# Top-32 attention with an MLP behind it: the order of the attention units changed, with the first loads and shifts moved

## Chip, cores and metric

One core of one Trainium2 chip. The metric is the device time of one execution in microseconds; the median of several executions is compared. All data is 32-bit float, except that the two weight matrices of the MLP arrive as 64-bit floats and are converted on the chip.

## The reference

Attention over 8 batches, 8 heads, 576 rows and head width 64, in which each row keeps only its 32 highest scores; then, on the joined heads (512 columns), a layer norm, a two-layer MLP (512 to 2048 to 512) and a residual:

```
scores = scale * np.matmul(q, k.transpose(0, 1, 3, 2))
kth = np.partition(scores, -top_k, axis=-1)[..., -top_k:-top_k + 1]
scores = np.where(scores >= kth, scores, -1000000000.0)
attn = softmax(scores)                       # max, exp, sum, divide
x = np.matmul(attn, v)                       # to (B, S, H*D)
xn = (x - mu) / np.sqrt(var + 1e-06) * g_ln
out = x + np.maximum(xn @ w_ch1, 0.0) @ w_ch2
```

## The kernel before, in words

**Units.** The attention is cut into units. A unit is one batch, one pair of heads (four pairs, `hp` 0 to 3) and one tile of query rows `qt`: tiles 0 to 3 have 128 rows for each of the two heads, tile 4 (`J`) is the rest, the last 64 rows, of which both heads share one tile of 128 partitions. There are 128 full units and 32 rest units, 160 in all. A `Job` is what one group of units of one head pair shares: keys and queries turned, values, one buffer `pt` of turned weights, one product with the values.

**The order of jobs** (L1027 to L1034) was: batch 0 as three parts (tiles 0 and 1; tiles 2 and 3; the rest alone), every part for the four head pairs; batch 1 as tiles 0, 1 and then tiles 2, 3 with the rest in the same group; batches 2 to 7 as tiles 0, 1 with the rest, then tiles 2, 3. So the rest units of batches 1 to 7 stood one by one between full units, and those of batch 0 as a run of four (units 16 to 19).

**Steps.** The main loop (from L1215) has one pass, a step, for each n. Each engine gets its instructions in exactly this written order (`manual_schedule`). Step n does, among other things:

- scores of unit n+2 on TensorE (L404), copied out of PSUM by ScalarE (`take_scores`, L385);
- the mask of unit n-1: ScalarE (L459, L460, L496), then GpSimd's subtraction (L499) and its watch (L466);
- the selection of the 32 highest of unit n on VectorE (`select`, MAX8 L447 and L439, MATCH_REPLACE8 L433), and at its end the halving of unit n+1 (L425, L426);
- the exponentials (L507) and the turning of the weights of a unit one or two steps back;
- the values of a group whose turned weights are complete (`values`, L632 and L639, `lag` steps after its last unit), and their placing into the rows of x (L674, L651);
- in between, eight times a step, `fill()`: pieces of MLP work from a list `todo`.

**Turning the weights.** A unit's 128-row weights reach `pt` in one of two ways. Either TensorE turns them (L565, eight transposes of 128x128 for a full unit, and two ScalarE copies at L577), or the unit is `moved`: VectorE turns blocks of 32x32 (L538, two instructions), one DMA writes them to DRAM (L553) and four bring them back in place (L548). The piece at the ends is turned by TensorE either way (L599). Before the change (L1058), of the units from the fifth job on, every unit that is not a rest and not the last of its group was moved.

**The MLP.** When four head pairs of two tiles are done, a block of 256 rows is given (`gives`): it is centred, turned (L738), multiplied by w1 (L779, 64 matmuls), and by w2. The first block uses plain products (L818); the 17 later ones a form with seven products for eight (L936, 56 matmuls), for which sums are made on GpSimd (L866 to L872) and two combined forms of w2 are fetched from DRAM (L1006). Two of the 18 blocks are made of rest rows, of four batches each. `slot(n)` spreads what is in `todo`, and what is to come, evenly over the steps left until the next gifts.

**Weights.** 32 pieces of w1 and w2 are fetched and converted in steps -1 to 19: ScalarE (L163, L165, L168), GpSimd (L164, L170), VectorE (`shift`, L176), GpSimd (`join`, L182, L184). The first four pieces were shifted and joined at the start of step 0, ahead of unit 0's selection on VectorE and ahead of everything that step gives GpSimd. MLP work on a weight piece can't start before it is joined. After the plain block the forms are built, so the projections of the second block can start at step 28.

**Loads.** Keys and queries of a job come by eight DMAs (L302): keys from SP's queue, queries, for the first two jobs, from ScalarE's. VectorE turns them (L331). A second job of the same batch and head pair (`twin`) fetches the turned keys and late queries that the first has kept in DRAM (`keep_heads` L345, `fetch_heads` L352); each job loads its values (L319), and GpSimd copies two pieces of them (`fill_ends`, L324).

Of the kernel before, what the change touches and what calls it, by code (L numbers as in the profile page):

```python
# [21 lines left out]
J = 4  # L22
# [7 lines left out]
def compute(  # L30
# [12 lines left out]
    nc = tc.nc  # L43
    P = nc.NUM_PARTITIONS
    B, H, S, D = q.shape
# [5 lines left out]
    NHP = H // 2  # L51
# [5 lines left out]
    def pool(name, bufs, **kw):  # L57
        return ctx.enter_context(tc.tile_pool(name=name, bufs=bufs, **kw))
# [23 lines left out]
    opool = pool("o", 2)  # L82
    xtpool = pool("xt", 1)
    hpool = pool("h", NF // 2)
    turnedpool = pool("turned_kq", 2, space=bass.MemoryType.DRAM)
    hbmpool = pool("hbm", 4, space=bass.MemoryType.DRAM)
    formpool = pool("forms", 1, space=bass.MemoryType.DRAM)
    psps = pool("ps", 5, space=PSUM)
# [111 lines left out]
    batches = {}  # L200
# [4 lines left out]
    batches = {n: x for n, x in batches.items() if x}  # L205
# [4 lines left out]
    def weights(n, phase):  # L210

        now, coming = batches.get(n, []), batches.get(n + 1, [])
        if phase == 0:
            for x in coming if n < LATE else []:
                x.fetch()
            for x in now[0::2] if n < LATE else []:
                x.split()
        elif phase == 1:  # L220
            for x in now if n >= LATE else now[1::2]:
                x.split()
            for x in coming if n >= LATE else []:
                x.fetch()

    def join_weights(n):
        for x in batches.get(n - 1, []):
            x.join()
# [65 lines left out]
    def load(job, first, second, later=False):  # L294

        job.ins = {}
        for name, src, queue in (("k", k, first), ("q", q, second)):
            t = ldpool.tile([P, S], FP32, tag=name + "in", name=name + "in")

            def part(i, t=t, src=src, queue=queue):  # L300
                head, d0 = 2 * job.hp + i * 32 // D, i * 32 % D
                queue.dma_start(  # L302
                    t[i * 32 : (i + 1) * 32, :].rearrange("b (n a) -> b n a", a=32),
                    src[job.b, head, :, d0 : d0 + 32].rearrange("(n b) a -> b n a", b=32),
                )

            for i in range(P // 32):
                if later:
                    age = (4 * len(job.ins) + i) // 2
                    loads.add(lambda i=i, part=part: part(i), -age)  # L310
                else:
                    part(i)
            job.ins[name] = t
# [62 lines left out]
    def scores(u):  # L376

        u.made = [score_half(u, s) for s in range(2)]
        return u.made[0][0][:, HALF:]

    def take_scores(u):
        u.sc = scpool.tile([P, 2, S], FP32, tag="sc", name="sc")
        for t in range(len(u.tiles)):
            for s in range(2):
                nc.scalar.copy(  # L385
                    u.sc[:, t, s * HALF : (s + 1) * HALF], u.made[s][t][:, 0:HALF]
                )
# [25 lines left out]
    def halve(u):  # L413

        nt = len(u.tiles)  # L420
        u.lo = lopool.tile([P, 2, HALF], FP32, tag="lo", name="lo")
        u.hi = hipool.tile([P, 2, HALF + 8 * low_rounds], FP32, tag="hi", name="hi")
        a, b = u.sc[:, 0:nt, 0:HALF], u.sc[:, 0:nt, HALF:S]
        lo, hi = u.lo[:, 0:nt], u.hi[:, 0:nt, 0:HALF]
        nc.vector.tensor_tensor(hi, a, b, ALU.max)  # L425
        nc.vector.tensor_tensor(lo, a, b, ALU.min)  # L426
# [66 lines left out]
    def mask(u, t):  # L493
        if u.e is None:
            u.e = epool.tile([P, 2, S], FP32, tag="e", name="e")
        nc.scalar.activation(  # L496
            u.e[:, t], u.sc[:, t], AF.Relu, bias=u.edge[:, t : t + 1], scale=-STEEP
        )
        nc.gpsimd.tensor_tensor(u.e[:, t], u.e[:, t], u.sc[:, t], ALU.subtract)  # L499
# [56 lines left out]
    def turn(u):  # L556

        g = u.group
        i0 = place_of(u)
        q0 = i0 * 32  # L560

        def part(t):
            ps = turned()
            for c in range(J):
                nc.tensor.transpose(  # L565
                    ps[:, c * P : (c + 1) * P], u.e[:, t, c * P + t * R : (c + 1) * P + t * R],
                    ident[:],
                )
            if u.rest:
                both = ps[:].rearrange("p (c h n) -> p h c n", h=2, n=R)  # L570
                for h in range(2):
                    nc.scalar.copy(
                        g.blocks[:, h, i0 : i0 + R // 32],
                        both[:, h].rearrange("p c (i n) -> p i c n", n=32),
                    )
            else:
                nc.scalar.copy(  # L577
                    g.blocks[:, t, i0 : i0 + P // 32],
                    ps[:].rearrange("p (c i n) -> p i c n", c=J, n=32),
                )  # L580

        def last():
            turn_ends(u)()

        heads = () if u.moved else range(len(u.tiles))
        return [lambda t=t: part(t) for t in heads] + [last]
# [58 lines left out]
    def take_values(g):  # L645
        g.oT = otpool.tile([P, GQ], FP32, tag="oT", name="oT")
        nc.scalar.copy(g.oT[:, 0 : g.nq], g.av[:, 0 : g.nq])
# [376 lines left out]

    jobs = []  # L1027
    for b in range(B):
        parts = [[0, 1], [2, 3], [J]]
        if b:  # L1030
            parts = [[0, 1], [2, 3]]
            parts[b < 2].append(J)
        for qts in parts:
            jobs += [Job(b, hp, [qts]) for hp in range(NHP)]  # L1034
    units = []
    for j in jobs:
        j.groups = [Group(j, qts) for qts in j.groups]
# [8 lines left out]
    fresh = []  # L1046
# [8 lines left out]
    CONVERTING = max(n for n in batches if batches[n]) + 2  # L1055
    EARLY = jobs[NHP].first

    for u in units[EARLY:]:  # L1058
        u.moved = not u.rest and u is not u.group.units[-1]


    for j, after_j in zip(jobs, jobs[1:] + [None]):
# [14 lines left out]
    for j in jobs:  # L1077
        if j.hp == NHP - 1:
            b = j.b
# [26 lines left out]
    def at(i):  # L1106
        return units[i] if 0 <= i < N else None
# [92 lines left out]
        x.fetch()  # L1200
    turn_heads(fresh[0])
    nc.sync.dma_start(grow[:], g_ln.rearrange("(c p) -> c p", p=P))
    load(fresh[1], nc.sync, nc.scalar)
    scores(units[0])
    take_scores(units[0])
    halve(units[0])
    scores(units[1])
    take_scores(units[1])
# [3 lines left out]
    for n in range(END):  # L1212
# [8 lines left out]
        u, nxt, mk = at(n), at(n + 1), at(n - 1)  # L1221
# [3 lines left out]
        parts = turn(ex) if ex and not ex.moved else []  # L1225
# [7 lines left out]
        if quick:  # L1233
            values(g)
            take_values(g)
        for x in batches.get(n - 1, []):
            x.shift()
        spare = None
        for x in ahead:
# [4 lines left out]
        if mk:  # L1244
            prepare(mk)
            for t in range(len(mk.tiles)):
                mask(mk, t)
        join_weights(n)
        if mk and doubt is not None:
            watch(mk)  # L1250
        if plain_done[0] is not None and plain_done[0] < n - 1:
# [85 lines left out]
        if last_rest and last_rest.rest and last_rest.job.b % 2:  # L1337
            hp = last_rest.job.hp
# [9 lines left out]
            select(u, 3)  # L1348
        if nxt:
            halve(nxt)  # L1350
        weights(n, 1)
        if g and not quick and g.job.hp == NHP - 1:
            for qt in g.qts:
# [18 lines left out]
@with_exitstack  # L1372
def kernel(
    ctx: ExitStack,
    tc: tile.TileContext,
    *operands: bass.AP,
):
    nc = tc.nc
    doubt = ctx.enter_context(tc.tile_pool(name="doubt", bufs=1)).tile(
        [1, 1], I32, tag="doubt", name="doubt"  # L1380
    )
    compute(tc, *operands, low_rounds=1, doubt=doubt[:])
    again = nc.values_load(  # L1383
        doubt[:], min_val=0, max_val=1,
        skip_runtime_bounds_check_because="a comparison's result",
    )
    with tc.If(again > 0):
        compute(tc, *operands, low_rounds=2, doubt=None)
# [31 lines left out]
```

## Time and profile before

Seen in one profiled execution on the chip; the medians are from executions without a profile.

| what | value |
|---|---|
| median of 3 runs (lowest, highest) | 1628.69 us (1627.76, 1628.86) |
| the profiled execution's own time | 1625.28 us |
| its span, first to last instruction | 1623.1 us |
| busy: TensorE matmul, VectorE, ScalarE, GpSimd | 1486.5, 1370.2, 1058.0, 1030.9 us |
| DMA | 228.27 MB, mean 141 GB/s |
| start of step 28 (VectorE's halving of unit 28) | 314.1 us |
| start of steps 40, 60, 88, 148 | 416.0, 584.3, 825.2, 1358.7 us |

How to read it: "PE" is TensorE's matmul, "PEld" its weight loads, "DVE" VectorE, "ACT" ScalarE, "POOL" GpSimd, "SP" SyncE. L936 is line 936 of the kernel. Each f32 matmul of the program stands as two records of TensorE, each transpose as one. The ends of matmuls are modelled, and one record lasts longer than the distance to the next start, so TensorE's busy time is more than the work that it did. The number in front of each step's time above is read from the VectorE instruction L425, of which there is one for each unit.

### The profile page before, as it was taken

Reading aid. Unit: us, or ns where it says so; the run is one execution under the profiler, and the core shown is the slowest. Engines: PE = TensorE matmul, PEld = TensorE weight load, DVE = VectorE, ACT = ScalarE, POOL = GpSimd, SP = SyncE. Lnnn points to the kernel's source line nnn. Section 1 sums busy time; section 2 is a strip of 40 time slices with the busy share of each in tenths; the row PEclk is TensorE's granted clock in tenths of the full one; section 3 lists DMA queues with packets and bytes.
Section 4 is the critical chain, followed back from the end, with each engine's and each line's share of the span. In section 5 each row is a group of like instructions: output and inputs, shape, how many; then the busy total and the mean of one; then the engine's idle time right before and its main releaser. Section 6 shows DMA issues by size and latency. Waiting matters only on the chain. (4 is left out here: it accounts for less than half of the span.)

```text
span 1623.1 us, 27069 instructions
## 1 busy us (share of the span) xinstructions
PE 1486.5 (92%) x7770; PEld 1124.5 (69%) x7770; DVE 1370.2 (84%) x3971; ACT 1058.0 (65%) x2984; POOL 1030.9 (64%) x1489
## 2 busy tenths in 40 slices
PE   3579678689979899999999999999999999999997
PEld 2346346467757677777777777777777777778886
DVE  5997978989999999999999999999999989882000
ACT  5878765566757686777666767677677766763221
POOL 6878976855546565667566747576657574746244
PEclk9779989799989999999999999999999999999999
DMA  6625644444646456445564556546554554522211
GB/s 159 167 69 160 195 119 130 153 138 118 197 121 202 126 144 172 158 152 133 162 192 131 142 148 176 161 122 174 144 174 149 146 148 156 157 90 85 71 34 54
DMA packets 367206, 228.27 MB, mean 141 GB/s; under 512 B 248772, under 2 KB 337352, under 8 KB 367048
## 3 DMA queue, kind: packets, MB, share of 16 engines
q1 hardware_dynamic: 362312, 225.86, 48.5%
q8 instruction: 64, 1.05, 0.3%
q10 hardware_dynamic: 4736, 0.59, 0.2%
q14 instruction: 94, 0.77, 0.2%
HBM read 154.01 MB, written 72.35 MB: 139 GB/s over the span
## 5 line engine op out<-in xcount | busy, mean ns | idle before, releaser
L499 POOL TENSOR_TENSOR e<-e,sc 128x576 f32<-128x576 f32 x288 | 405.1, 1425 | 421.7 <-ACT e L496 323.9
L779 PE MATMUL hps<-xT,w 128*128 128x256 f32 x2304 | 542.1, 385 | 6.0 <-ACT xT L741 3.8
L779 PEld LDWEIGHTS hps<-xT,w 128*128 128x128 f32 x2304 | 430.3, 193 | 76.2 <-issue 10.8
L447 DVE MAX8 m<-hi 128x8 f32<-128x296 f32 (+1 forms) x1152 | 469.8, 442 | 0.1
L433 DVE MATCH_REPLACE8 hi<-m,hi 128x288 f32<-128x288 f32 (+1 forms) x864 | 377.1, 441 | 0.0
L936 PE MATMUL ops<-w,h 128*128 128x256 f32 x1360 | 322.4, 384 | 3.4 <-DMA w<-forms 3.4
L936 PEld LDWEIGHTS ops<-w,h 128*128 128x128 f32 x1360 | 254.0, 193 | 41.7 <-issue 5.0
L496 ACT ACTIVATE e<-sc,m 128x576 f32<-128x576 f32 x288 | 209.3, 769 | 90.1 <-PE scps L599 89.0
L507 ACT ACTIVATE e<-e,m 128x576 f32<-128x576 f32 x288 | 226.8, 790 | 32.3 <-POOL e L499 31.3
L385 ACT COPY sc<-scps 128x288 f32<-128x288 f32 x576 | 187.0, 402 | 63.3 <-POOL e L499 49.8
L425 DVE TENSOR_TENSOR hi<-sc 128x576 f32<-128x576 f32 (+1 forms) x160 | 134.3, 840 | 68.4 <-POOL watched L466 64.0
L802 ACT ACTIVATE h<-hps 128x512 f32<-128x512 f32 x144 | 87.3, 607 | 121.3 <-PE hps L779 120.7
L632 PE MATMUL av<-pt,vb 128*64 128x256 f32 (+2 forms) x1088 | 143.2, 405 | 0.8 <-ACT pt L604 0.6
L426 DVE TENSOR_TENSOR lo<-sc 128x576 f32<-128x576 f32 (+1 forms) x160 | 135.4, 846 | 0.0
L538 DVE STREAM_TRANSPOSE sc<-e 128x512 f32<-128x512 f32 x176 | 113.9, 682 | 22.3 <-ACT e L507 22.3
L404 PE MATMUL scps<-kT,late_qT 64*128 64x288 f32 (+3 forms) x832 | 123.4, 415 | 7.8 <-ACT sc L385 5.7
L936 PE MATMUL ops<-wt,s 128*128 128x256 f32 x544 | 128.7, 381 | 0.4 <-POOL s L866 0.4
L439 DVE MAX8 hi<-lo 128x8 f32<-128x288 f32 x288 | 117.5, 443 | 0.0
L404 PE MATMUL scps<-kT,qT 64*128 64x288 f32 x512 | 91.7, 470 | 24.8 <-DVE qT L331 23.5
L565 PE MATMUL tp<-ident,e 128*128 128x128 f32 x448 | 73.3, 291 | 44.6 <-ACT e L507 29.7
L936 PEld LDWEIGHTS ops<-wt,s 128*128 128x128 f32 x544 | 100.1, 190 | 16.0 <-issue 2.3
L404 PEld LDWEIGHTS scps<-kT,late_qT 64*128 64x128 f32 (+1 forms) x832 | 70.6, 169 | 58.0 <-issue 18.0
(107 smaller groups left out, 1846.5 us busy)
## 6 DMA issues: line engine op xcount, KB each, us to landing
turned<-sc SPq DMA_DIRECT2D x88, 512.0 KB, 2.9
pt<-turned SPq DMA_DIRECT2D x352, 128.0 KB, 2.8
w<-forms SPq DMA_DIRECT2D x136, 256.0 KB, 4.1
vb<-in_v_dram SPq DMA_DIRECT2D x68, 288.0 KB, 3.6
raw<-in_moe_w_ch_dram SPq DMA_DIRECT2D x32, 512.0 KB, 5.3
kT<-kept SPq DMA_DIRECT2D x36, 288.0 KB, 3.3
kin<-in_k_dram SPq DMA_DIRECT2D x128, 72.0 KB, 2.6
kept<-kT SPq DMA_DIRECT2D x32, 288.0 KB, 3.0
```

The lines of the kernel that those rows point to most:

```text
L385: nc.scalar.copy(u.sc[:, t, s * HALF : (s + 1) * HALF], u.made[s][t][:, 0:HALF])
L404: nc.tensor.matmul(ps[i * R : i * R + ql, o : o + width], qT[r, q0 : q0 + ql], kT[r, k0 : k0 + width], start=True, stop=True,)
L425: nc.vector.tensor_tensor(hi, a, b, ALU.max)
L426: nc.vector.tensor_tensor(lo, a, b, ALU.min)
L433: nc.vector.match_replace(x, m[:, t, :], x, LOWEST)
L447: nc.vector.max(m[:, t, :], u.hi[:, t, 0:width])
L496: nc.scalar.activation(u.e[:, t], u.sc[:, t], AF.Relu, bias=u.edge[:, t : t + 1], scale=-STEEP)
L499: nc.gpsimd.tensor_tensor(u.e[:, t], u.e[:, t], u.sc[:, t], ALU.subtract)
L507: nc.scalar.activation(u.e[:, t], u.e[:, t], AF.Exp, bias=u.bias[:, t : t + 1], scale=-scale, accum_out=g.den[:, col : col + 1],)
L632: nc.tensor.matmul(av[h * D : (h + 1) * D, 0 : g.nq], vb[:, h * (J + 1) + c, :], g.blocks[:, h, 0 : g.nq // 32, c, :], start=(c == 0), sto ...
L779: nc.tensor.matmul(ps[0][:, side * N : (side + 1) * N], w1[:, c, f * P : (f + 1) * P], self.xT[:, c, 0:N], start=(c == 0), stop=(c == NC - 1),
L936: nc.tensor.matmul(bank[name][:, 0:Q], a(j), rhs, start=first and j == 0, stop=(j == G - 1), skip_group_check=not first,)
```

## The change

- The order of jobs is written out. The rest rows of batches 0, 1, 2 and 3 are jobs of their own (runs of four rest units), and each run stands one or more parts behind its batch: batch 0's behind tiles 0, 1 of batch 2, batch 1's behind tiles 0, 1 of batch 3, batch 2's behind tiles 2, 3 of batch 3, batch 3's behind tiles 0, 1 of batch 4. Batches 4 and 5 have the rest with tiles 2, 3; batches 6 and 7 with tiles 0, 1, and the tiles 2, 3 of batches 6 and 7 come last.
- From the third batch on, the last unit of a group is moved as well (turned by VectorE), unless the next group begins with a rest unit, or it is a rest itself. The number of moved units goes from 88 to 103.
- Five instead of two DRAM buffers hold the kept keys and late queries of each head pair.
- The second job's loads are issued after the scores of unit 0 are copied, not before.
- The first four weight pieces are shifted and joined at the end of step 0, not at its start.

```diff
-    turnedpool = pool("turned_kq", 2, space=bass.MemoryType.DRAM)
+    turnedpool = pool("turned_kq", 5, space=bass.MemoryType.DRAM)
...
-    jobs = []
-    for b in range(B):
-        parts = [[0, 1], [2, 3], [J]]
-        if b:
-            parts = [[0, 1], [2, 3]]
-            parts[b < 2].append(J)
-        for qts in parts:
-            jobs += [Job(b, hp, [qts]) for hp in range(NHP)]
+    rows, rest = ([0, 1], [2, 3]), [J]
+    order = [(0, rows[0]), (0, rows[1]), (1, rows[0]), (1, rows[1])]
+    order += [(2, rows[0]), (0, rest), (2, rows[1]), (3, rows[0]), (1, rest)]
+    order += [(3, rows[1]), (2, rest), (4, rows[0]), (3, rest), (4, rows[1] + rest)]
+    order += [(5, rows[0]), (5, rows[1] + rest)]
+    order += [(6, rows[0] + rest), (7, rows[0] + rest), (6, rows[1]), (7, rows[1])]
+    assert B == 8
+    jobs = [Job(b, hp, [qts]) for b, qts in order for hp in range(NHP)]
...
-    for u in units[EARLY:]:
-        u.moved = not u.rest and u is not u.group.units[-1]
+    for j, nj in zip(jobs, jobs[1:] + [None]):
+        for u in units[max(j.first, EARLY) : j.last + 1]:
+            u.moved = not u.rest and (
+                u.i < j.last or (j.b > 1) and nj is not None and not units[nj.first].rest
+            )
...
-    load(fresh[1], nc.sync, nc.scalar)
     scores(units[0])
     take_scores(units[0])
+    load(fresh[1], nc.sync, nc.scalar)
...
-        for x in batches.get(n - 1, []):
+        for x in batches.get(n - 1, []) if n else []:
             x.shift()
...
-        join_weights(n)
+        if n:
+            join_weights(n)
...
         if nxt:
             halve(nxt)
+        if n == 0:
+            for x in batches[-1]:
+                x.shift()
+            join_weights(0)
         weights(n, 1)
```

## The prediction

> **What bounds the kernel now.** I read first the page's table of busy times and its forty slices: no engine is full over the whole span, TensorE (PE) is full from about slice 15 on, and VectorE (DVE) goes idle at slice 37.
>
> ```profile
> PE 1486.5 (92%) x7770; PEld 1124.5 (69%) x7770; DVE 1370.2 (84%) x3971; ACT 1058.0 (65%) x2984; POOL 1030.9 (64%) x1489
> PE   3579678689979899999999999999999999999997
> DVE  5997978989999999999999999999999989882000
> PEclk9779989799989999999999999999999999999999
> ```
>
> Second, the table by windows, cut at the starts of steps 28, 40, 60, 88 and 148 (columns: length, busy time of PE, PEld, DVE, ACT, POOL, granted clock, DMA share, GB/s).
>
> ```profile
> 314.10:416.00 101.90, 93.42 (x491) 69.88 (x491) 93.97 (x276) 69.15 (x206) 58.75 (x89) 0.93 0.48 145
> 416.00:584.30 168.30, 152.66 (x799) 112.66 (x796) 165.23 (x492) 114.50 (x338) 95.48 (x145) 0.95 0.56 158
> 584.30:825.20 240.90, 238.40 (x1302) 182.79 (x1302) 235.73 (x697) 170.28 (x502) 153.96 (x238) 1.00 0.55 155
> 825.20:1358.70 533.50, 532.20 (x2884) 410.38 (x2883) 505.75 (x1478) 373.13 (x1077) 345.61 (x525) 1.00 0.53 153
> 1358.70:1623.10 264.40, 253.34 (x1276) 208.67 (x1274) 105.14 (x312) 110.56 (x294) 131.19 (x223) 0.99 0.29 88
> ```
>
> Steps 28 to 60 are VectorE's (92 and 98% busy); then both are nearly full; at the end TensorE works alone. Third, since a matmul's busy time is modelled, TensorE's timeline, for the distance between starts:
>
> ```profile
> 1013.64 2.38 PE L632 MATMUL av<-pt,vb 128*64 128x320 f32 x16
> 1015.94 0.81 PE L639 MATMUL av<-pt,ends 128*128 128x320 f32 x2
> 1016.59 3.18 PE L936 MATMUL ops<-w,h 128*128 128x256 f32 x14
> ...
> 1559.49 1.04 PE L738 MATMUL tp<-ident,x 128*128 128x128 f32 x8
> 1560.36 0.60 PE L936 MATMUL ops<-w,h 128*128 128x256 f32 x2
> 1561.25 27.89 PE L779 MATMUL hps<-xT,w 128*128 128x256 f32 x128 [0.29 <-ACT xT L741]
> 1588.98 10.52 PE L936 MATMUL ops<-w,h 128*128 128x256 f32 x48
> ```
>
> 128 records in 27.73 us are 0.2166 us each, so 0.433 a matmul; a transpose is 0.87 / 8 = 0.109; a values product of 320 rows takes 2.95. Read in the same way, one of 256 rows takes 2.41 and one of 64 rows (at 216.7 us) 0.88; a score matmul 0.293. Priced so, TensorE's work from step 28 on is 1239.8 us (442.9 hidden, 411.7 projections, 151.0 scores, 145.1 values, 34.1 transposes L565, 55.0 others), while those steps took 1309.0. By stage: 85.5, 148.5, 232.9, 523.7, 249.1. So from step 60 to 148 TensorE is at 97 to 98% of that price: it is the bound there, whereas steps 28 to 60 hold 36 us in which it starves.
>
> **What the skill says.** "Perfetto Trace Analysis", Identifying the Most-Contended Engine: matmul busy time is a poor measure. The trace agrees: 532.20 of 533.50 us is shown against 523.7 priced by starts. "TensorE: Matmul & The Clock Gate", What's actually happening: an idle TensorE falls to half clock. The trace agrees in kind: 0.93 and 0.95 in the two starving stages, 1.00 after. "SBUF — State Buffer", Who interferes with whom: VectorE instructions with two SBUF inputs and GpSimd reads lock each other out. The trace agrees in kind: L425 takes 0.99 us at 314.1, 0.73 at 323.5. That is why I scale VectorE.
>
> **The change, part by part.** The order in which the changed kernel issues its instructions gives the counts.
>
> *Turned by VectorE.* 15 more units: TensorE loses 120 transposes, 120 x 0.109 = 13.1 us, ScalarE 30 copies (0.587 us each, 17.6 us; it has room), VectorE gains 30 transposes L538 at 0.678 (18 to 20 us), SP 75 DMAs (15 MB).
>
> *Rests alone.* Twelve groups of 320 rows become 256 and 64: 2.41 + 0.88 - 2.95 = 0.34 us, 4 us on TensorE. GpSimd gains 24 copies L324 at 0.23 us (6 us, hidden: it is 65% busy). SP's queue gains 36 loads (kept keys, late queries, values; 9 MB). With the other DMAs SP has 111 more, 24 MB on 228; DMA share 0.53 in the middle, so I take nothing. What stands behind SP's waits is later loads, issued two steps ahead; if that cover goes, each late load costs up to its landing, about 3 us, and TensorE waits. `fill_ends` waits on TensorE's previous values, with the next mask behind it on GpSimd; before, this was seen once with a 3.6 us wait on TensorE.
>
> *Sum on TensorE from step 28:* 1228.9, which is 10.9 less.
>
> *Order.* Steps 16 to 19 were rests and become full units. Before, those took 41.5 us (186.0 to 227.5), the four full steps ahead of them 47.8 (138.2 to 186.0): +6.3. Two key turnings (1.4 us each) move ahead into steps 13 and 15; most of that returns later: +2. VectorE's extra work in steps 0 to 27 is 17.9 us, which is the upper end; zero the lower.
>
> *Early moves.* Queries' four DMA issues (2.99 us on ScalarE) no longer stand ahead of the first copies, and VectorE no longer waits for four shifts (it idles 7 us in step 0). But unit 2's halving waits for GpSimd's watch of unit 0 (40.3 us), which stands behind the same eight joins (10 us) as before. The gain is capped there: I take 1, bounds 0 and 7. New wait: joins behind the late shifts, with unit 0's masks behind them; GpSimd has piece five's two instructions meanwhile. Five DRAM buffers cost nothing: space alone.
>
> So step 28 starts at 314.1 + 6.3 + 2 - 1 = 321.4.
>
> *Stages from there.* VectorE's work before, priced by starts, was 88.3, 158.6, 224.5, 476.2 and its busy time 1.065, 1.042, 1.050, 1.062 times that; I keep the factors. TensorE gets 1.018 (533.5 / 523.7).
>
> - Steps 28 to 39: VectorE 109.5 x 1.065 = 116.6, TensorE 104.6. VectorE decides: 116.6.
> - 40 to 59: VectorE 162.7 x 1.042 = 169.5, TensorE 165.5; they alternate (four rests, then sixteen full units), so a little over: 171.
> - 60 to 87: TensorE 231.3 x 1.018 = 235.5, VectorE 206.
> - 88 to 147: TensorE 487, VectorE 470 x 1.062 = 499, but TensorE enters it behind, up to two steps; 492.
> - From 148: TensorE 251.8 against 249.1; 264.4 + 2.8 = 267.2.
>
> Sum 1282.3 for 1309.0. The span is 321.4 + 1282.3 = 1603.7; the time lay 2.2 above the span, so 1605.9 where the profiled run had 1625.3; the median lies 3.4 above that one: **1609**.
>
> What is late next is VectorE itself: its stages are within 3% of TensorE's.
>
> **The rivals.**
>
> *The front costs nothing* (full steps no slower, factors 1.04): 314 + 114 + 169 + 235.5 + 488.5 + 265 = 1586, so 1592. For it: the rests' steps 19 and 20 took 14.1 and 12.1 us, with stalls. Against: VectorE has 17.9 us more in there.
>
> *Stretches add instead of overlapping: slower.* A rest step wants some 9 us of TensorE and 4.8 of VectorE, a full step the reverse. One can run ahead only two steps (scores of n+2, the watch of n-2). If that doesn't bridge runs of four, each stretch costs its larger side: 116.6 + (37 + 150.6) + (110 + 143.7) + 499 + 267 = 1324, so 1651. Half of this surplus over my forecast gives 1630, the time before; beyond half it decides. I take 1640 for this case. For it: singles between full units are smoother. Against: the two-step slack is some 16 us, and a run's surplus is 16.
>
> *Nothing measurable*: the front at its upper end and half that surplus cancel: 1628.
>
> **How the numbers follow.** Forecast (1598 to 1622) 0.50; free front 0.20, 1592; same 0.08, 1628; adding stretches 0.22, 1640. A difference under 0.2% (3 us) can't be told from none. Faster 0.70, same 0.08, slower 0.22. For 8 in 10 the range goes from 1586 to 1638.
>
> **What would show it.** Right: step 28 starting at 316 to 327; VectorE's idle time and TensorE's gaps in steps 40 to 88 small, clock 1.00; steps 28 to 148 near 1015 us against 1044.5; L565 with 328 records, L538 with 206. Wrong: step 28 at 310 or 335; TensorE gaps of 3 us and more next to each rest run, with GpSimd L324 or a kept key as releaser.

## The result, and the profile after

The changed kernel takes 1634.36 us (median of 5 runs, 1630.87 to 1636.99). The kernel before, run beside it, takes 1627.76 us (1626.18 to 1628.86). The ratio is 1.0039, with a 95% interval of 1.0027 to 1.0052: slower by 0.4%, where 1609 and a gain of 1.2% were forecast. The profiled execution of after has a time of 1630.87 us, the fastest of the five, and a span of 1628.8 us; of before 1625.28 and 1623.1. So the traces show 5.7 us of the 6.6 between the medians.

The page of after: busy times and two of the forty-slice rows.

```profile
PE 1479.2 (91%) x7866; PEld 1124.5 (69%) x7866; DVE 1383.3 (85%) x4001; ACT 1045.4 (64%) x2966; POOL 1036.8 (64%) x1513
PE   3578779799899989999899999999999999999997
DVE  5997998999979997998978999999999999767200
```

TensorE has less to do and VectorE more, as the change says. By busy times alone it looks like an improvement. The table by windows of after, cut at the starts of steps 28, 40, 60, 88 and 148 (columns as in the prediction), says where the time is.

```profile
318.50:430.40 111.90, 106.07 (x572) 81.74 (x573) 111.76 (x335) 74.85 (x214) 71.82 (x110) 0.98 0.64 179
430.40:615.10 184.70, 172.67 (x966) 132.71 (x965) 172.75 (x497) 121.37 (x357) 109.35 (x171) 0.97 0.62 179
615.10:854.40 239.30, 229.98 (x1398) 179.56 (x1397) 210.98 (x614) 161.63 (x482) 146.85 (x232) 1.00 0.60 171
854.40:1355.80 501.40, 494.42 (x2678) 377.32 (x2677) 490.13 (x1444) 350.08 (x1037) 316.38 (x498) 1.00 0.58 166
1355.80:1628.80 273.00, 256.48 (x1277) 210.66 (x1276) 121.59 (x346) 108.69 (x290) 138.88 (x230) 0.98 0.35 110
```

In steps 40 to 59 (second line) neither engine is full: of 184.7 us TensorE is busy for 172.67 and VectorE for 172.75, so each lacks 12 us. Something else holds both. The view of waits shows what it is. First before (who waited, for whom: us in total, times, longest):

```profile
DVE hi L425 <- POOL watched L466: 64.0, 41, 5.1
PE xo L674 <- ACT oT L647: 3.5, 4, 1.6
ACT sc L385 <- DMA turned<-sc: 0.5, 1, 0.5
```

Then after:

```profile
DVE hi L425 <- POOL watched L466: 101.6, 42, 8.7
ACT sc L385 <- DMA turned<-sc: 40.0, 24, 5.0
PE xo L674 <- ACT oT L647: 22.1, 16, 3.3
```

ScalarE's copying of scores (L385) waits for the transfer `turned<-sc` 24 times instead of once, 40.0 us in all, and TensorE waits 22.1 us for a copy of ScalarE (L647) instead of 3.5. The first row, the largest, misleads: it is 101.6 us in the new order even where the time is 25 us better (first experiment).

One such wait in the timeline of after (start, length, engine, line, operation; in brackets the idle time ahead and what ended it):

```profile
545.00 1.28 DVE L538 STREAM_TRANSPOSE sc<-e 128x512 f32<-128x512 f32 x2
546.86 0.42 SPq L553 DMA_DIRECT2D turned<-sc  x1
...
552.56 1.31 ACT L385 COPY sc<-scps 128x288 f32<-128x288 f32 x4 [3.85 <-DMA turned<-sc]
554.21 0.42 ACT L647 COPY oT<-av 128x256 f32<-128x256 f32 x1
...
554.69 0.69 PE L674 MATMUL xo<-ident,oT 128*128 128x128 f32 x2 [3.15 <-ACT oT L647]
```

The chain can be read off. `move` turns the weights of unit u in step u+2 and writes the result into that unit's own score tile `sc` (L538, its last record ending at 546.28). The store L553 reads it from there (issued 546.86). The pool of score tiles has five buffers, so unit u+5, whose scores are copied in step u+3, gets the same buffer, and L385 has to wait until the store has landed (552.56). ScalarE works in order, so the copy L647, ready earlier, comes only at 554.21, and TensorE, whose next instruction places the values (L674), stands still for 3.15 us. The Trainium skill ("Perfetto Trace Analysis", Tensor Engine Instruction (MATMUL, LD_WEIGHTS)) calls the execution queues of ScalarE, VectorE and GpSimd strict FIFOs; these lines agree: nothing of ScalarE passed the waiting copy in 3.85 us. In steps 28 to 147 TensorE is idle for 34 us in all (the first four lines of the table above: 5.8, 12.0, 9.3 and 7.0), and 20.1 us of it are waits of L674 for L647.

### The profile page after: what moved, and what is told of

It is laid out like the page before. It is cut to its first block, busy times and chain, and to the rows that moved or that the text cites. A ratio compares the mean times of both kernels' runs of the same rounds, so it can differ in the third digit from the quotient of the medians.

```text
span 1628.8 us, 27486 instructions
## 1 busy us (share of the span) xinstructions
PE 1479.2 (91%) x7866; PEld 1124.5 (69%) x7866; DVE 1383.3 (85%) x4001; ACT 1045.4 (64%) x2966; POOL 1036.8 (64%) x1513
## 4 chain that ended last, share of the span: by engine, by line
PE 45%; DVE 32%; POOL 9%; ACT 6%; DMA 5%; issue 2%; SPq 0%; ACTq 0%; DVEq 0%; POOLq 0%
PE hps L779 19%; PE ops L936 13%; DVE m L447 10%; DVE hi L433 8%; PE scps L404 5%; PE av L632 4%; DVE sc L538 3%; POOL e L499 3%; DVE lo L426 3%; DVE hi L425 3%; DMA turned<-sc 3%; DVE hi L439 2%; PE av L639 1%; PE tp L565 1%; ACT sc L385 1%
## 5 line engine op out<-in xcount | busy, mean ns | idle before, releaser
L499 POOL TENSOR_TENSOR e<-e,sc 128x576 f32<-128x576 f32 x288 | 408.5, 1437 | 456.3 <-ACT e L496 334.7
L385 ACT COPY sc<-scps 128x288 f32<-128x288 f32 x576 | 188.0, 403 | 86.9 <-DMA turned<-sc 40.0
L425 DVE TENSOR_TENSOR hi<-sc 128x576 f32<-128x576 f32 (+1 forms) x160 | 134.1, 838 | 104.7 <-POOL watched L466 101.6
L632 PE MATMUL av<-pt,vb 128*64 128x256 f32 (+2 forms) x1280 | 145.7, 370 | 9.8 <-DMA pt<-turned 5.7
L538 DVE STREAM_TRANSPOSE sc<-e 128x512 f32<-128x512 f32 x206 | 133.3, 682 | 10.8 <-ACT e L507 6.4
L632 PEld LDWEIGHTS av<-pt,vb 128*64 128x64 f32 x1280 | 80.7, 139 | 58.4 <-issue 15.1
```

The source lines that it names most:

```text
L385: nc.scalar.copy(u.sc[:, t, s * HALF : (s + 1) * HALF], u.made[s][t][:, 0:HALF])
L632: nc.tensor.matmul(av[h * D : (h + 1) * D, 0 : g.nq], vb[:, h * (J + 1) + c, :], g.blocks[:, h, 0 : g.nq // 32, c, :], start=(c == 0), sto ...
```

## The experiments

Theory A: the additional moves are what costs, through the reuse of the score tile behind a late store. Theory B is the rival that the prediction had priced: runs of four rest units and the long stretches of full units add up instead of overlapping. Medians are in us; ratios are against the kernel before, run beside each. After was not run again beside them, and the median of before lies between 1625.96 and 1627.76 from series to series; so a difference between two kernels of different series is known to some 2 us only. Taken against before in each series, the loss of 24.7 below is 23.8, and the gain of 17.2 is 16.3.

**The order alone** (`e1_order_only`). The new order stays; the rule for moved units is the old one (76 moved), and the first loads and shifts are where they were.

```diff
-    for j, nj in zip(jobs, jobs[1:] + [None]):
-        for u in units[max(j.first, EARLY) : j.last + 1]:
-            u.moved = not u.rest and (
-                u.i < j.last or (j.b > 1) and nj is not None and not units[nj.first].rest
-            )
+    for u in units[EARLY:]:
+        u.moved = not u.rest and u is not u.group.units[-1]
```

> The new order of jobs alone: the old rule for moving (units that are not the last of their group, 76 of them), the old first loads and shifts. Theory A (the 27 last units that are moved as well cost the time: with every unit moved, ScalarE's copy of scores waits for the DMA that still reads the same buffer, and TensorE behind it): faster than the changed kernel by 8 to 20 us, so 1614 to 1626, with ScalarE's wait of L385 for the DMA turned<-sc falling from 40 to under 15 us. Theory B (the runs of four rest units cost it: VectorE and TensorE can't run ahead of each other far enough, so the stretches add): no faster than the changed kernel, 1634 to 1650, since TensorE also gets 27 x 8 transposes back (23 us of its work).

Measured: 1609.66 (1608.47 to 1611.64), ratio 0.9891 (0.9873 to 0.9909). The order by itself gains 1.1%. L385 doesn't wait for a store at all, and steps 40 to 59 have a full TensorE at full clock (172.99 busy of 173.9):

```profile
317.10:426.80 109.70, 109.70 (x595) 84.97 (x596) 108.68 (x328) 78.36 (x224) 71.11 (x107) 0.97 0.61 168
426.80:600.70 173.90, 172.99 (x1022) 134.58 (x1020) 163.08 (x483) 127.92 (x366) 111.36 (x175) 1.00 0.52 147
600.70:836.10 235.40, 235.40 (x1449) 183.90 (x1448) 205.59 (x602) 169.47 (x497) 146.62 (x232) 1.00 0.50 142
836.10:1334.40 498.30, 494.99 (x2708) 378.00 (x2707) 484.77 (x1434) 353.14 (x1041) 316.55 (x498) 1.00 0.56 159
```

Over these four stages TensorE is idle for 4 us, against 28 in before and 34 in after. Its waits, for the two rows that after has too:

```profile
DVE hi L425 <- POOL watched L466: 101.6, 44, 9.6
PE xo L674 <- ACT oT L647: 4.6, 7, 1.8
```

B falls: the runs of four are all there, and the kernel is faster than before. It is faster than A's 1614 to 1626 as well, so the moves cost more than A expected. The 27 further moves (103 less 76) and the front together turn 1609.66 into 1634.36, a loss of 24.7.

**The moved rule alone** (`e2_moved_only`). The kernel before with the new rule only, in the old order (111 moved, 23 more).

> The new rule for moving alone, in the old order with the old first loads and shifts: 111 moved units for 88. Theory A: slower than the kernel before by 5 to 20 us (1633 to 1648), and the wait of L385 for the DMA turned<-sc appears. Theory B: as before or faster by up to 10 us (1618 to 1628), since TensorE, the bound from step 60 on, loses 23 x 0.87 = 20 us of transposes.

Measured: 1633.96 (1631.44 to 1636.14), ratio 1.0042 (1.0025 to 1.0058). The rule costs in the old order too, here 7 us, and the same wait appears:

```profile
ACT sc L385 <- DMA turned<-sc: 19.1, 20, 3.4
PE xo L674 <- ACT oT L647: 14.6, 11, 3.4
```

The loss is smaller than in the new order. A possible reason, not tested: where TensorE and its scores are late themselves, they cover a part of the store.

**The move earlier in the step** (`e3_move_early`). The whole change, but `move` runs ahead of the selection's second part instead of after the third, so L538 and its store come about 4 us sooner: L538 ends 4.2 us after the start of the halving that precedes it, where after has 8.4 (medians over the moved units). No instruction is added or taken away.

```diff
+        if moved:
+            move(ex)
         if u:
             select(u, 1)
...
             select(u, 2)
         for blk, i in rows_of.pop(n, []):
             blk.stats(i)
-        if moved:
-            move(ex)
```

> The changed kernel with VectorE's two transposes of a moved unit placed ahead of the second selection round of the step, not behind the third, so that the store to DRAM starts about 4 us sooner and has landed before the score buffer is wanted again. Nothing else changes. Theory A: the wait of L385 for the DMA turned<-sc falls below 10 us and the kernel is faster than the changed one by 5 to 15 us, 1620 to 1629. Theory B: within 3 us of the changed kernel, 1631 to 1637.

Measured: 1617.15 (1613.63 to 1619.3), ratio 0.9943 (0.9927 to 0.9958): 17.2 less than after, with the same work. The gain is larger than A's 5 to 15, and the wait of L385, 13.2 us where it was 40.0, stays above A's 10. TensorE's idle time in steps 28 to 147 falls from 34 to 21 us, and the part of it that waits for L647 from 20.1 to 12.4:

```profile
ACT sc L385 <- DMA turned<-sc: 13.2, 10, 4.0
PE xo L674 <- ACT oT L647: 14.7, 14, 2.5
```

**The early place where no store is late** (`e6_order_early`, `e8_before_early`). The same edit on the order alone and on the kernel before tells whether the early place is good in itself.

> The new order with the old rule for moving and old front, and the move ahead of the second selection round. In the run without the early place L385 never waits for the store, so if the early place gains by taking that wait away, there is nothing to gain here: 1606 to 1612. If it gains in another way (the bring back to pt is sooner, VectorE's work lies better), it gains here as well: 1595 to 1603.

> The kernel before with the move ahead of the second selection round. There L385 waited for the store 0.5 us in all, so by the theory of the late store nothing is gained: 1624 to 1629. A gain of 5 us or more would say that the early place helps by itself.

Measured: 1612.81 (1609.87 to 1614.17) for the order, a little above the 1606 to 1612 expected and 3.2 more than without the edit; 1626.58 (1624.57 to 1629.68) for before, ratio 1.0000 (0.9992 to 1.0008). Where no store is late, the place gains nothing, so the gain of e3 comes with the late stores. It also gives the price of the 27 moves (with the new front) without most of that wait: 1617.15 less 1612.81, 4.3 us.

One rival is left out by this pair. Neither kernel moves the last unit of a group, so neither shows what a sooner bringing back is worth where a group's product with the values (L632) has to wait for its last unit's blocks. By the traces it is small: TensorE waits at L632 for `pt<-turned` for 5.7 us in after (twice), 3.2 in e3 (once) and not at all in the order alone. So it is a second cost of the moves, and it can account for some 2.5 us of the gain.

**Half-way** (`e7_move_mid`). The whole change with `move` ahead of the selection's third part, one round of some 1.7 us sooner.

```diff
+        if moved:
+            move(ex)
         if u:
             select(u, 2)
...
-        if moved:
-            move(ex)
```

> The changed kernel with the move one selection round sooner (1.7 us) than it stands, half as far as in the run with the move early. If the time is set by how late the store lands, half the effect or more: 1622 to 1629, with 15 to 30 us of L385 waiting for turned<-sc. If it needs the whole distance, or the cause is another, 1632 to 1636.

Measured: 1626.79, but its 14 runs spread from 1621.21 to 1634.03; ratio 1.0004 (0.9991 to 1.0016). That is 7.6 less than after, and L385's wait is 32.2 us (15 to 30 were expected). With the two others of 103 moves this gives an order: waits of 40.0, 32.2 and 13.2 us, times of 1634.4, 1626.8 and 1617.2. The waits are from one execution each, so the order carries weight, the slope (0.6 us of time for each us of wait) little.

**Rests as singles** (`e4_singles`). The whole change, but each run of four rests is broken up: for each head pair the full job and the rest that follows it in the list come together. This takes 12 moves away as well, since the rule leaves out a unit ahead of a rest (91 moved).

```diff
-    jobs = [Job(b, hp, [qts]) for b, qts in order for hp in range(NHP)]
+    jobs, i = [], 0
+    while i < len(order):
+        pair = order[i : i + 1 + (i + 1 < len(order) and order[i + 1][1] == rest)]
+        jobs += [Job(b, hp, [qts]) for hp in range(NHP) for b, qts in pair]
+        i += len(pair)
```

> The changed kernel with each run of four rest units broken up: each of the four rests stands behind one job of the part that it follows, so full and rest units alternate 2 to 1 as in the old order. The last units of those parts are then not moved (the next group begins with a rest): 12 moved units fewer. Theory B: VectorE's idle time in steps 32 to 88 falls by at least half and the kernel is faster than the changed one by 10 to 20 us, 1614 to 1625. Theory A: faster only by the share of moves taken away (12 of 27), 4 to 8 us, 1626 to 1631.

Measured: 1628.52 (1623.98 to 1633.02, 22 runs), ratio 1.0012 (1.0003 to 1.0020): 5.8 less than after. A share of 12 in 27 moves of the loss of 24.7 would be 11. L385's wait is 22.3 us in 13 times, so A has its part. B's own sign is not there: VectorE's idle time in steps 32 to 87 is 45.5 us, in after 40.3, where B wanted it halved. What breaking the runs adds or takes can't be read from this run alone.

**The order with the new front** (`e5_order_front`). The whole change with the old moved rule: against e1 it adds the re-timed loads and shifts.

> The changed kernel with the old rule for moving (76 units); against the run of the new order alone it adds the late loads of the second job and the late first shifts and joins. If the front is capped by GpSimd's joins, as the prediction had it, within 3 us of that run (1607 to 1613). If the shifts were a cost of their own, 5 us or more away from it on either side.

Measured: 1611.21 (1610.98 to 1612.19), ratio 0.9909 (0.9896 to 0.9922), against 1609.66 (1608.47 to 1611.64) without the front. The ranges overlap; the new front gains nothing. Its mechanism is the one forecast: VectorE starts sooner (halving of unit 1 at 19.2 us in after, 29.1 in before), but then unit 2's halving waits 8.7 us for GpSimd, whose eight joins (L182, L184) stand ahead of unit 0's subtraction (L499) and watch (L466). GpSimd's timeline in after:

```profile
25.60 1.26 POOL L182 TENSOR_TENSOR size<-size,wt 128x512 uint32<-128x512 uint32 x1
...
35.86 2.75 POOL L499 TENSOR_TENSOR e<-e,sc 128x576 f32<-128x576 f32 x2
...
41.14 0.19 POOL L466 TENSOR_TENSOR watched<-hi,m 128x2 f32<-128x2 f32 x1
```

The watch comes at 41.14 us, in before at 40.3, and the halving of unit 2 starts at 41.4, in before at 42.0.

**Where the moves cost** (`e10_head_moves`, `e9_tail_moves`). Two kernels on top of the order alone: one has the additional moves only in batches 2 to 5 (20 of the 27), the other only in batches 6 and 7 (the other 7), where TensorE works nearly alone.

```diff
-    u.i < j.last or (j.b > 1) and nj is not None and not units[nj.first].rest
+    u.i < j.last or (1 < j.b < 6) and nj is not None and not units[nj.first].rest
```

```diff
-    u.i < j.last or (j.b > 1) and nj is not None and not units[nj.first].rest
+    u.i < j.last or (j.b > 5) and nj is not None and not units[nj.first].rest
```

> The same with the new rule in batches 2 to 5 alone: the other 20 of the 27 last units, in steps 32 to 112. If the cost sits where VectorE is the bound, nearly the whole of it is here: 1630 to 1640, with 35 us or more of L385 waiting for turned<-sc. If it is spread by number: 20 of 27 parts of 25 us, 1626 to 1630.

> The new order, the old front, and the new rule for moving in batches 6 and 7 alone: 7 of the 27 last units, all from step 144 on, where TensorE works through 11 units of cost a step and VectorE waits. If the store costs only where ScalarE gets to the copy early, that is where VectorE is the bound, these moves cost nothing and TensorE is spared 7 x 0.87 = 6 us: 1602 to 1609, L385 not waiting for turned<-sc. If a late store costs wherever it stands: 1612 to 1618.

Measured: 1633.67 (1632.42 to 1636.35) with the 20, ratio 1.0049 (1.0035 to 1.0062), as slow as the whole change; 1610.38 (1609.99 to 1612.22) with the 7, ratio 0.9906 (0.9891 to 0.9921). The waits of the first, then of the second:

```profile
ACT sc L385 <- DMA turned<-sc: 36.1, 19, 4.4
PE xo L674 <- ACT oT L647: 21.7, 15, 3.0
```

```profile
PE xo L674 <- ACT oT L647: 4.5, 7, 1.8
ACT sc L385 <- DMA turned<-sc: 1.5, 2, 1.3
```

All the loss is made in batches 2 to 5, where VectorE has little room beside a full TensorE (in the order alone it is busy 94% of steps 40 to 59 and 87% of 60 to 87). After against the order alone, stage by stage from step 28, is 2.2, 10.8, 3.9 and 3.1 us longer and, from step 148, 2.4 shorter. In the last batches the 7 moves cost nothing; the time lies between the two ranges expected. Of the 7 x 0.87 = 6 us of transposes that they take from TensorE, some 2.3 show in the traces from step 148 on (273.1 us against 275.4 in the order alone), and nothing in the medians.

**Which stores are late.** Setting each L385 of after beside the store of the unit five earlier gives: 7 of the 24 waits (7.9 us) are for stores of units moved additionally; 15 (29.3 us) for the unit right behind such a one; 2 (2.8 us) for others. In the order alone none of the 76 stores is waited for. So the store of a unit that was moved before as well becomes late when the unit ahead of it is moved too. The landing of the store, 2.6, 2.9 and 6.0 us in before (lowest, median, highest), is 2.6, 3.2 and 7.3 in after; for the 20 units of batches 2 to 5 right behind an additional one it is 4.8 in the median, and for the same 20 units 2.7 in the order alone.

The four transfers that bring the predecessor's blocks back are not what these stores share the engines with: 21 of the 24 have a landing on record, 20 of these follow a moved unit, and in 18 all of that unit's landings on record came before the store was issued (in the lines above at 545.72 us at the latest, and the store at 546.86). In flight beside the stores of the 20 units of batches 2 to 5 are mostly values, kept keys and forms of w2, in all (each transfer counted whole) some 0.9 MB on average in after, 0.3 in the order alone. These stand in SP's queue behind the bringing back, and the queue waits at its start (L548) until the predecessor's own store has landed. After, then the order alone:

```profile
SPq L548 <- DMA turned<-sc: 254.8, 95, 6.9
```

```profile
SPq L548 <- DMA turned<-sc: 171.4, 71, 5.7
```

That this wait pushes the other loads into the next store fits these numbers; it wasn't tried by itself.

**Not tried.** A sixth score buffer would move the reuse a unit further away.

The best version is e1_order_only: 1609.66 us, 1.1% below before.

## Why the prediction was wrong

What was expected of the order came about, though the prediction never priced it alone; what was forecast for the moves was wrong. The span came out at 1628.8, 25.1 above the predicted 1603.7; by stage, measured less forecast: up to step 28 -2.9, steps 28 to 39 -4.7, 40 to 59 +13.7, 60 to 87 +3.8, 88 to 147 +9.4, from 148 +5.8.

- *Turned by VectorE*: **this step failed.** It counted 120 transposes fewer on TensorE, more VectorE work and 75 more DMAs on SP, and took nothing for the DMAs ("so I take nothing", under *Rests alone*) because only later loads stand behind SP's waits. Its counts are right (L565 has 328 records, L538 206), and the store itself is seldom issued late: L553 follows L538 by 0.03 us in the median, and by under 0.2 in 19 of the 24 late cases. What it didn't follow is the buffer that the transfer reads. The wait that costs is not on the queue that issues the DMA but on ScalarE, which rewrites `sc` five units later, and behind ScalarE stands TensorE. Its price for a late transfer ("about 3 us, and TensorE waits") was put at loads. Turning and storing the same units sooner, in e3, gave back 17.2 us of the loss of 24.7, and e6 and e8 show that the early place gives nothing where the stores aren't late; without the 27 moves, in e1, wait and loss are both gone.
- *The work of the moves*, apart from the wait: with the early place the 27 moves still cost 4.3 us instead of saving. They give VectorE 27 x 1.36 = 37 us and take 27 x 0.87 = 23.5 from TensorE. The prediction had this work in its stages, but it summed order and moves together and never asked what the new order would give without the further moves; so it didn't see that they add to VectorE in the very stages (28 to 59) in which its own sums had VectorE as the longest. In steps 40 to 59 VectorE was put at 169.5 and is busy 172.75 in after; the other 12 of the 184.7 us are idle.
- *The order*: right in kind. With the old moved rule TensorE's starving is gone (idle 4 us in steps 28 to 147, 28 in before), and steps 40 to 59 and 60 to 87 take 173.9 and 235.4 us, where 171 and 235.5 were forecast for the whole change. That the order alone ends at 1609.66, the very number forecast, is in part luck: it has 23.5 us more of TensorE's work and 37 less of VectorE's than the forecast counted.
- *Order at the front and early moves*: step 28 starts at 318.5, forecast 321.4. The order alone delays it by 3.0 us (317.1 after 314.1), where 6.3 + 2 were forecast; the gain of the early moves is capped by GpSimd's joins as said (1 us forecast; e5, at 318.2, shows none).
- *Steps 28 to 148*: forecast 1015, measured 1037.3, in the order alone 1017.3. *From 148*: forecast 267.2, measured 273.0 in after and 275.4 in e1, 264.4 before. So the new order's end takes 6 to 8 us more than was forecast, with or without the moves. This wasn't resolved.
- *Rival of adding stretches*: it had the sign (1640) and even steps 40 to 59 (37 + 150.6 = 187.6 against 184.7), yet it is not the cause: e1 has the same stretches, and there that stage takes 173.9 us. The near number came from a wrong mechanism. In the case *nothing measurable* the sum is off as well: half of this surplus alone gave 1630 there, so with a dearer front beside it the time would lie above 1628.
- *What would show it*: "TensorE gaps of 3 us and more" was right as a sign, but the releaser is ScalarE's L647 behind a store, not L324 or a kept key.

What stays open: which part of the 4.3 us is VectorE's work, which the 13.2 us of wait that e3 still has and which the 3.2 us at L632; why the tail's moves gain so little; and whether the stores land late because SP's waits push other loads beside them.

## What to carry to other kernels

When a change adds a DMA, ask not only what is queued behind it, but which buffer it reads or writes, how many units later that buffer comes round again, which engine rewrites it, and what stands behind that instruction. Where two engines lack the same time in a stage, as here in steps 40 to 59, look for what holds both: here it was a wait whose count jumped from 1 to 24, not the largest one. Try the parts of a change one by one: here one part gained 17 us and another lost some 24.

## What the runs showed of the hardware

In after, a store of 128 x 1024 floats (512 KB) landed after 2.6 us at best, 3.2 in the median and 7.3 at worst, with the DMA engines 0.58 to 0.64 busy in steps 28 to 147. The stores that ScalarE waited for took 4.0 us in the median, the others 3.0, so here the slow part of the landings decided when a buffer came free, more than their median. Placing the two VectorE instructions of each moved unit 4 us earlier, with no instruction changed, was worth 17.2 us, and nothing in the two kernels in which next to no store was waited for (0.5 us in before, none in the order alone).
